# Decode attention with a gated MLP: early sum copied ahead of the late blocks, a share of the last key product on GpSimd, programs aligned to a block

## The chip, the cores and the metric

The kernel runs on one core of a Trainium2 chip. The metric is the device time of one execution in microseconds; the kernel before took 677.2 us (median of 3 runs, 676.89 to 677.97). A core has TensorE (PE) for matrix products, VectorE (DVE), ScalarE (ACT), GpSimd (POOL) and SyncE (SP), which here issues nearly all transfers. Sixteen DMA engines move the data from HBM into the on-chip memory SBUF; PE writes its sums to PSUM banks.

## The reference

Two inputs of one token each (B = 2, width 448) go through two branches that share x. Branch A is attention with a cache, branch B a two-layer MLP with a squared ReLU:

```python
q = (x @ wq).reshape(B, 1, 16, 256).transpose(0, 2, 1, 3)
scores = einsum("bhqd,bhkd->bhqk", q, k_cache) * 256 ** -0.5   # 4096 keys a head
o = einsum("bhqk,bhkd->bhqd", softmax(scores), v_cache)
a = o.transpose(0, 2, 1, 3).reshape(B, 1, 4096) @ wo
b = relu(x @ w1 + b1) ** 2 @ w2 + b2
g = sigmoid((x * gate_w).sum(-1, keepdims=True))
return g * a + (1 - g) * b
```

All is float32. The two caches are 2 x 16 x 4096 x 256 values each, 134 MB each; wq, wo, w1 and w2 are small beside them.

## The kernel before

**Rounds.** The attention goes in 16 rounds `r`, one for each pair of heads `t` (8) and each batch entry `b` (2). A round has 8.4 MB of keys and as much of values, laid over 128 partitions: 64 partitions a head, and 64 keys of 256 values (`KEYS` = 64, `DH` = 256) in each partition. The buffers are `keys[0]`, `keys[1]` (alternating) and `vals`.

**VectorE** (its loop is written out, L206 to L245): in each round it multiplies the keys in place with the broadcast query (L213), sums each product over 256 (the reduce of L222, 64 scores per partition), takes the maximum per partition (L223) and, after PE has spread it, over the head (L224). Between product and reduce stand two small steps for the round before (`normed`, L196 to L200). ScalarE then takes the exponentials (L240) into `p8` and the row sums. Ahead of the first rounds VectorE also does small steps for the gate and the hidden layer.

**PE** (L328 to the end, its own program): the gate's sum, q, the first layer of branch B (`fin`, L353 to L362), its transposes (L363 to L368), then the second layer summed into the bank `acc` by `add` (L371 to L374). A loop of 15 passes (L378 to L383) takes, for each round, the values times the exponentials into `po` (`values`, 32 calls), the scaling and turning of the result (`turn`), which ScalarE copies to `oT`, the next round's maxima and sums. The sixteenth round follows the loop (L386 to L390), because its values come in two parts into `keys[0]` (`V_CUT` = 48 of the 64 keys, semaphores `VT`).

**The last product, with wo** (L391 to L410). wo is 32 blocks of 128 x 448, loaded into `vals` in five cuts (`WO_CUTS` = 0, 16, 24, 28, 31, 32; semaphores `WL`), as soon as PE has read the values of the last round but one. The first 24 blocks ("early", 32 - `LATE`) go into the same bank `acc` as branch B, two columns wide, by `add`. Then ScalarE copies the sum to `ya` (L260). The last 8 blocks ("late") go to the bank `fin`, with the output's 448 columns split over four groups of PE's columns (`late`, four calls each); their left operands are copied by VectorE into the wide, zero-filled tile `wide` (L257 to L259). Halfway through the late blocks (`n == LATE // 2`), PE adds the early sum, by multiplying `ya` with the selection matrix `pick`. VectorE copies `fin` to `y4` (L261), and SP writes it out (L264).

**The order of the transfers** is that of SP's program: wq, the keys of round 0, the weights of branch B, then keys and values in turn, each waiting until its buffer has been read; at the end the last round's values, then the five cuts of wo. All of them go through one queue, so they land in that order.

GpSimd only sets up small tiles at the start and clears semaphores at the end (L266 to L270).

Of the kernel before, what the change touches and what calls it, by code (L numbers as in the profile page):

```python
# [7 lines left out]
ALU = mybir.AluOpType  # L8
AX = mybir.AxisListType

P = 128
WO_ORDER = [0, 1, 2, 3, 7, 4, 5, 6]
LATE = 8
WO_CUTS = (0, 16, 24, 28, 31, 32)
V_CUT = 48


class Count:
# [16 lines left out]
def gated_mix_kernel(nc, b2, wq, wf, wo, k_cache, v_cache, out):  # L35
    B, H, S, DH = k_cache.shape
# [5 lines left out]
    KEYS = 2 * S // P  # L42
# [11 lines left out]
    pe, dve, act, pool, sp = nc.tensor, nc.vector, nc.scalar, nc.gpsimd, nc.sync  # L54
    rounds = [(t, b) for t in range(T) for b in range(B)]
    R = len(rounds)

    def sb(name, *free):
        return nc.alloc_sbuf_tensor(name, [P, *free], F32)[:]
# [12 lines left out]
    pick = sb("pick", W)  # L72
    wide = sb("wide", LATE, W)
    p8 = sb("p", NM, 4)
# [12 lines left out]
    ya = sb("ya", D)  # L87
# [6 lines left out]
    DV, AC, TE, GP = (Count(nc, n) for n in ("dve", "act", "pe", "pool"))  # L94
    KL = [Count(nc, "k0_landed"), Count(nc, "k1_landed")]
# [14 lines left out]
    def kv(cache, r):  # L110
        t, b = rounds[r]
        return cache[b, 2 * t:2 * t + 2].rearrange("h (p j) d -> (h p) (j d)", j=KEYS)

    def load(dst, src, sem, after=None):
        ins = sp.dma_start(dst, src)  # L115
        if after:
            after[0].on(ins, after[1])
        return sem.up(ins, 16)
# [10 lines left out]
    def te_mt(r):  # L129
        return TE_MT0 if r == 0 else TE_SUM0 + 4 * (r - 1) + 3  # L130

    def te_sum(r):
        return TE_SUM0 if r == 0 else TE_SUM0 + 4 * (r - 1) + 4

    def te_val(r):
        return TE_SUM0 + 4 * r + 1

    def te_ot(r):
        return TE_SUM0 + 4 * r + 2

    TE_ACC = te_ot(R - 1) + 1
    TE_FIN = TE_ACC + 1


    pool.memset(ident, 0.0)
    GP.up(pool.memset(ones, 1.0))
# [37 lines left out]
    AC_QB = [AC.up(TE.on(act.activation(qb[:, i, :], QBANK[i % 4], AF.Copy), TE_QB[i])) for i in range(T * B // 2)]  # L184
# [6 lines left out]
    def turned(r):  # L191
        t, b = rounds[r]
        OC.up(TE.on(act.activation(o, po, AF.Copy), te_val(r)))  # L193
        AC_OT[r] = AC.up(TE.on(act.activation(oT[:, t, :, b, :], ot[:, :NJ * 2].rearrange("p (j h) -> p j h", h=2), AF.Copy), te_ot(r)))  # L194

    def normed(r):  # L196
        b = rounds[r][1]
        n = DV.up(TE.on(dve.reciprocal(rc, sm[:, :2]), te_sum(r)))
        RL.up(DV.on(dve.scalar_tensor_tensor(rl, rc.unsqueeze(1).to_broadcast([P, 2, 2]), gP[:, 0, b:b + 1],
                                             sel.rearrange("p (s h) -> p s h", s=2), op0=ALU.mult, op1=ALU.mult), n))  # L200

    def k_view(r):
        return keys[r % 2].rearrange("p (j d) -> p j d", d=DH)

    load(keys[1], kv(k_cache, 1), KL[1], (TE, TE_Q1))
    for r, (t, b) in enumerate(rounds):  # L206
        kt = k_view(r)
        q = qb[:, (t // 2) * B + b, (t % 2) * DH:(t % 2 + 1) * DH]
        if r < 4:
            dve.wait_ge(AC.h, AC_QB[(t // 2) * B + b])  # L210
        elif r == 4:
            dve.wait_ge(AC.h, AC_QB[-1])
        n = DV.up(KL[r % 2].on(dve.tensor_tensor(kt, kt, q.unsqueeze(1).to_broadcast([P, KEYS, DH]), op=ALU.mult), 16 * (r // 2 + 1)))  # L213
        if r == 0:
            DV_H = DV.up(TE.on(dve.tensor_tensor(hb, sm[:, :FC * B].rearrange("p (c b) -> p c b", b=B), b1T.unsqueeze(2).to_broadcast([P, FC, B]), op=ALU.add), TE_PT))
            DV_H = DV.up(DV.on(dve.tensor_scalar(hb, hb, 0.0, None, op0=ALU.max), DV_H))
            DV_H = DV.up(DV.on(dve.tensor_mul(hT, hb, hb), DV_H))
            DV_H = DV.up(DV.on(dve.tensor_tensor(hT, hT, gP[:, 1, :].unsqueeze(1).to_broadcast([P, FC, B]), op=ALU.mult), DV_H))
            load(vals, kv(v_cache, 0), VL, (TE, TE_ADD))
        else:  # L220
            normed(r - 1)
        DV_S = DV.up(DV.on(dve.tensor_reduce(s, kt, axis=AX.X, op=ALU.add), n))  # L222
        MX.up(DV.on(dve.tensor_reduce(m, s, axis=AX.X, op=ALU.max), DV_S))  # L223
        DV_NB = DV.up(TE.on(dve.tensor_reduce(nb, mt[:, :64], axis=AX.X, op=ALU.max, negate=True), te_mt(r)))  # L224
        if r > 0:
            turned(r - 1)
            if r < R - 1:
                load(vals, kv(v_cache, r), VL, (TE, te_val(r - 1)))
            else:
                for i, (lo, hi) in enumerate(zip(WO_CUTS, WO_CUTS[1:])):  # L230
                    load(vals[:, lo * D:hi * D], wo[:, lo * D:hi * D], WL[i], (TE, te_val(r - 1)) if i == 0 else None)
        if r + 2 < R:
            load(keys[r % 2], kv(k_cache, r + 2), KL[r % 2], (DV, DV_S))
        elif r + 2 == R:
            at = V_CUT * DH
            load(keys[r % 2][:, :at], kv(v_cache, R - 1)[:, :at], VT[0], (DV, DV_S))
            load(keys[r % 2][:, at:], kv(v_cache, R - 1)[:, at:], VT[1])
        for hh in range(2):
            z = slice(64 * hh, 64 * hh + 64)
            e = act.activation(p8[z, :, hh:hh + 3:2], s[z].rearrange("p (m s) -> p m s", s=2), AF.Exp,  # L240
                               bias=nb[z], accum_out=rsm[z, hh:hh + 1])
            if hh == 0:
                DV.on(e, DV_NB)
            else:
                EX.up(e)  # L245
# [3 lines left out]
    blocks = [(t, k) for t in WO_ORDER for k in range(4)]  # L249
    early = len(blocks) - LATE  # L250

    def o_block(t, k):
        hh, j = divmod(k, 2)
        return oT[:, t, j, :, hh]

    dve.wait_ge(AC.h, AC_OT[R - 1])
    for n, (t, k) in enumerate(blocks[early:]):  # L257
        DV_W = dve.tensor_copy(wide[:, n, 0:W:16], o_block(t, k))  # L258
    DV_W = DV.up(DV_W)  # L259
    AC_YA = AC.up(TE.on(act.activation(ya, acc[:, :D], AF.Copy), TE_ACC))  # L260
# [12 lines left out]
    def mm(dst, lt, rhs, start=True, stop=True):  # L273
        return pe.matmul(dst, lt, rhs, start=start, stop=stop)  # L274
# [7 lines left out]
    def done(ins, n):  # L282
        ins.then_inc(TE.h, 1)
        te[0] += 1
        assert te[0] == n, (te[0], n)

    def values(v, lo=0, hi=NM):
        vv = v.rearrange("p (m s d) -> p m (s d)", s=2, d=DH)
        for i in range(lo, hi):
            g = 32 * (i % 4)  # L290
            ins = mm(po[g:g + 4, :], p8[:, i, :], vv[:, i, :], i < 4, i >= NM - 4)
        return ins

    def turn():
        take(OC)
        take(RL)
        for j in range(NJ):
            for x in range(2):
                at = x * DH + j * P
                ins = mm(ot[:, j * 2:j * 2 + 2], o[:, at:at + P], rl[:, x, :], x == 0, x == 1)  # L300
        return ins
# [11 lines left out]

    n_acc = 1 + FC + T * 4 - LATE
    added = [0]

    def add(lt, rhs):
        n = added[0]
        g = 32 * (n % 4)
        added[0] += 1  # L320
        return mm(acc[g:g + B, :D], lt, rhs, n < 4, n >= n_acc - 4)

    def late(lt, rhs, start=False, stop=False):
        for k in range(4):
            ins = mm(fin[32 * k:32 * k + W, :DQ], lt, rhs[:, k * DQ:(k + 1) * DQ], start, stop)
        return ins
# [5 lines left out]
    for c in range(CF + 1):  # L332
        for n in range(4 * QW):
# [3 lines left out]
            else:  # L337
                half, i = divmod(n, 2 * QW)
                lt, at = xT[:, CF + half, :], CF * N + i * QB
            ins = mm(pq[a][32 * gq:32 * gq + B, :], lt, wqt[:, at:at + QB], c == 0, c == CF)  # L340
# [13 lines left out]
    for c in range(CF + 1):  # L354
        for n in range(4):
            if c < CF:
                lt, at = xT[:, c, :], c * F + n * D
            else:
                half, i = divmod(n, 2)
                lt, at = xT[:, CF + half, :], CF * F + i * D  # L360
            ins = mm(fin[32 * n:32 * n + B, :D], lt, vals[:, at:at + D], c == 0, c == CF)
# [4 lines left out]
    for n in range(2):  # L366
        ins = mm(sm[64 * n:64 * n + 64, CF * 8:CF * 8 + 4], hs[:, CF * P:D], rows[:, 2 * n:2 * n + 2, :B])
# [4 lines left out]
    for c in range(FC):  # L372
        ins = add(hT[:, c, :], vals[:, w2_at + c * D:w2_at + (c + 1) * D])
# [12 lines left out]
    pe.wait_ge(VT[0].h, 16)  # L386
    values(keys[R % 2], 0, V_CUT // 2)
    pe.wait_ge(VT[1].h, 16)
    done(values(keys[R % 2], V_CUT // 2, NM), te_val(R - 1))
    done(turn(), te_ot(R - 1))  # L390
    pe.wait_ge(AC.h, AC_OT[R - 1])  # L391
    i_w = 0
    for i, (t, k) in enumerate(blocks):
        if i == WO_CUTS[i_w]:
            pe.wait_ge(WL[i_w].h, 16)
            i_w += 1
        rhs = vals[:, i * D:(i + 1) * D]
        if i < early:
            ins = add(o_block(t, k), rhs)
            if i == early - 1:  # L400
                done(ins, TE_ACC)
            continue
        n = i - early
        if n == 0:
            pe.wait_ge(DV.h, DV_W)
        if n == LATE // 2:
            pe.wait_ge(AC.h, AC_YA)
            late(pick, ya)
        ins = late(wide[:, n, :], rhs, n == 0, n == LATE - 1)
    done(ins, TE_FIN)  # L410


# [63 lines left out]
```

## Time and profile before

| | |
|---|---|
| median of 3 runs (lowest, highest) | 677.2 us (676.89, 677.97) |
| the profiled execution, its own time | 676.97 us |
| its span, first to last instruction | 675.6 us |
| TensorE clock granted, mean | 0.653 |
| VectorE busy | 566.4 us, 84% |
| PE busy | 215.6 us, 32% |
| ACT, POOL busy | 36.2 us, 2.1 us |
| read from HBM | 289.55 MB, 429 GB/s over the span |

The profile is of one execution. Its times are microseconds from the start of the span unless marked ns. A row of the timeline gives start, length, engine, source line, operation, what it writes and reads, how often (x), and in brackets the idle time of the engine before it with what ended that. L274 and L115 are lines of helpers (`mm`, `load`), so their rows are told apart by the tiles. PEld is PE's loading of weights. Queue q1 carries the kernel's data; queues of the kind "instruction" carry program code to the engines.

### The profile page before, as it was taken

What the parts mean: (1) busy time and instruction counts of PE and PEld (TensorE: products, weight loads), DVE (VectorE), ACT (ScalarE), POOL (GpSimd) and SP (SyncE); (2) the same over time, 40 slices, a digit from 0 to 9 for tenths busy, and PEclk for the clock granted to TensorE, in tenths of its full rate; (3) what the DMA queues carried; (4) which work ended last, traced back from release to release, by engine and by line L of the source; (5) the groups of instructions that cost most, each with busy time, mean ns of one, the idle gap of its engine ahead of it and who ended that gap; (6) DMA issues with size and microseconds to landing.
All of it is one profiled execution on the core that took longest, in us unless ns stands there. A gap on an engine that the chain in (4) does not pass through costs nothing. (4 is left out here: it accounts for less than half of the span.)

```text
span 675.6 us, 3473 instructions
## 1 busy us (share of the span) xinstructions
PE 215.6 (32%) x1522; PEld 67.6 (10%) x1522; DVE 566.4 (84%) x120; ACT 36.2 (5%) x111; POOL 2.1 (0%) x15
## 2 busy tenths in 40 slices
PE   0726141150605124060503305050421405051357
PEld 0201000010101101010100101010010101011012
DVE  1066999999989797998979798997979799797960
ACT  0121000000000000000000000000000000000000
POOL 1000000000000000000000000000000000000000
PEclk9976666575756657585755658575565858565579
DMA  9999999999999999999999999999999999999997
GB/s 381 431 453 421 435 435 436 435 431 435 435 435 435 435 431 435 435 435 435 435 435 435 435 435 435 431 435 435 435 431 435 435 435 435 435 435 435 423 418 293
DMA packets 5779, 289.63 MB, mean 429 GB/s; under 512 B 653, under 2 KB 782, under 8 KB 1038
## 3 DMA queue, kind: packets, MB, share of 16 engines
q1 hardware_dynamic: 5772, 289.56, 99.2%
q8 instruction: 3, 0.05, 0.0%
q14 instruction: 2, 0.02, 0.0%
q10 hardware_dynamic: 2, 0.00, 0.0%
HBM read 289.55 MB, written 0.00 MB: 429 GB/s over the span
## 5 line engine op out<-in xcount | busy, mean ns | idle before, releaser
L213 DVE TENSOR_TENSOR k<-k,q 128x16384 f32<-128x16384 f32 x16 | 275.6, 17223 | 51.7 <-DMA k<-in_k_cache_dram 51.7
L222 DVE TENSOR_REDUCE s<-k 128x64 f32<-128x16384 f32 x16 | 275.4, 17212 | 0.0
L274 PE MATMUL po<-v,p 128*4 128x512 f32 x960 | 137.4, 737 | 291.4 <-PEq L278 291.4
L274 PEld LDWEIGHTS po<-v,p 128*4 128x4 f32 x960 | 26.6, 99 | 389.5 <-issue 389.5
L274 PE MATMUL mt<-ident,m 128*64 128x64 f32 x64 | 7.7, 334 | 88.8 <-PEq L278 88.8
L193 ACT ACTIVATE o<-po 128x512 f32<-128x512 f32 x16 | 9.6, 597 | 449.8 <-PE po L274 449.8
L274 PE MATMUL ot<-rl,o 128*128 128x2 f32 x128 | 16.4, 250 | 15.6 <-PEq L278 15.6
L274 PEld LDWEIGHTS ot<-rl,o 128*128 128x128 f32 x128 | 15.5, 191 | 30.0 <-issue 30.0
L240 ACT ACTIVATE p<-s,nb 64x64 f32<-64x64 f32 x32 | 11.2, 350 | 104.8 <-DVE nb L224 104.6
L274 PE MATMUL sm<-rsm,ones 128*128 128x2 f32 x32 | 8.9, 348 | 21.2 <-PEq L278 21.2
L274 PEld LDWEIGHTS mt<-ident,m 128*64 128x64 f32 x64 | 5.2, 205 | 90.4 <-issue 90.4
L174 DVE COPY pk<-k 128x28 f32<-128x28 f32 x1 | 0.2, 179 | 16.5 <-DMA k<-in_wq_dram 16.5
L224 DVE TENSOR_REDUCE nb<-mt 128x1 f32<-128x64 f32 x16 | 3.6, 224 | 10.6 <-PE mt L274 10.6
L274 PE MATMUL fin<-v,pk 128*2 128x448 f32 x32 | 6.0, 933 | 16.6 <-DMA v<-in_wf_dram 16.6
L274 PEld LDWEIGHTS sm<-rsm,ones 128*128 128x128 f32 x32 | 8.0, 310 | 23.8 <-issue 23.8
L258 DVE COPY wide<-oT 128x2 f32<-128x2 f32 x8 | 0.7, 162 | 10.4 <-ACT oT L194 10.4
L274 PE MATMUL pq<-k,pk 128*2 128x512 f32 x64 | 9.3, 747 | 0.0
L274 PE MATMUL po<-k,p 128*4 128x512 f32 x64 | 8.7, 702 | 0.0
L274 PE MATMUL sm<-ys,ones 128*128 128x2 f32 x2 | 0.6, 350 | 21.0 <-DVE ys L177 21.0
L261 DVE COPY y<-fin 128x112 f32<-128x112 f32 x1 | 0.3, 275 | 7.7 <-PE fin L274 7.7
L240 ACT ACTIVATION_READ_ACCUMULATOR p<-s,nb 64x1 f32 x32 | 5.9, 184 | 0.0
L274 PE MATMUL acc<-v,oT 128*2 128x448 f32 x48 | 4.9, 538 | 0.4 <-ACT oT L194 0.3
(59 smaller groups left out, 58.2 us busy)
## 6 DMA issues: line engine op xcount, KB each, us to landing
k<-in_wq_dram SPq DMA_DIRECT2D x1, 7182.0 KB, 19.6
v<-in_wf_dram SPq DMA_DIRECT2D x1, 6272.0 KB, 52.8
k<-in_v_cache_dram SPq DMA_DIRECT2D x1, 6144.0 KB, 37.8
v<-in_wo_dram SPq DMA_DIRECT2D x1, 3584.0 KB, 18.6
k<-in_v_cache_dram SPq DMA_DIRECT2D x1, 2048.0 KB, 42.4
v<-in_wo_dram SPq DMA_DIRECT2D x1, 1792.0 KB, 22.6
v<-in_wo_dram SPq DMA_DIRECT2D x1, 896.0 KB, 24.3
v<-in_wo_dram SPq DMA_DIRECT2D x1, 672.0 KB, 25.4
```

The source lines that it names most:

```text
L174: DV_PK = DV.up(QL.on(dve.tensor_copy(pk, keys[1][:, 3 * N + N // 2:3 * N + N // 2 + PK]), 16))
L193: OC.up(TE.on(act.activation(o, po, AF.Copy), te_val(r)))
L213: n = DV.up(KL[r % 2].on(dve.tensor_tensor(kt, kt, q.unsqueeze(1).to_broadcast([P, KEYS, DH]), op=ALU.mult), 16 * (r // 2 + 1)))
L222: DV_S = DV.up(DV.on(dve.tensor_reduce(s, kt, axis=AX.X, op=ALU.add), n))
L224: DV_NB = DV.up(TE.on(dve.tensor_reduce(nb, mt[:, :64], axis=AX.X, op=ALU.max, negate=True), te_mt(r)))
L240: e = act.activation(p8[z, :, hh:hh + 3:2], s[z].rearrange("p (m s) -> p m s", s=2), AF.Exp, bias=nb[z], accum_out=rsm[z, hh:hh + 1])
L258: DV_W = dve.tensor_copy(wide[:, n, 0:W:16], o_block(t, k))
L261: DV_Y4 = DV.up(TE.on(dve.tensor_copy(y4, fin[:, :DQ]), TE_FIN))
L274: return pe.matmul(dst, lt, rhs, start=start, stop=stop)
```

## The change

Three edits, told apart here as part 1, 2 and 3.

Part 1: `LATE` goes from 8 to 4, so 28 blocks are early. PE waits for the copy `ya` and multiplies it with `pick` ahead of the first late block, not halfway; that product now opens the sum in `fin`. The wait for VectorE's copies into `wide` stands right behind the last early block.

Part 2: in the last round (r = 15) VectorE multiplies 54 of the 64 keys, GpSimd the other 10 (`HELP`), both released by the keys' landing. VectorE's reduce waits for GpSimd.

Part 3: a directive at the head of PE's program puts its next instruction on a boundary of 256 instructions, and one at the head of VectorE's on a boundary of 128; `max_nops=0` has the program branch over the padding.

```diff
-LATE = 8
+LATE = 4
...
+HELP = 10
...
+    dve.addr_align(128, 0, max_nops=0)
+    pe.addr_align(256, 0, max_nops=0)
...
-        n = DV.up(KL[r % 2].on(dve.tensor_tensor(kt, kt, q.unsqueeze(1).to_broadcast([P, KEYS, DH]), op=ALU.mult), 16 * (r // 2 + 1)))
+        own = KEYS if r < R - 1 else KEYS - HELP
+
+        def times_q(e, lo, hi):
+            return KL[r % 2].on(e.tensor_tensor(kt[:, lo:hi], kt[:, lo:hi], q.unsqueeze(1).to_broadcast([P, hi - lo, DH]), op=ALU.mult), 16 * (r // 2 + 1))
+
+        n = DV.up(times_q(dve, 0, own))
+        if own < KEYS:
+            pool.wait_ge(AC.h, AC_QB[-1])
+            GP_HELP = GP.up(times_q(pool, own, KEYS))
...
             normed(r - 1)
+        if own < KEYS:
+            dve.wait_ge(GP.h, GP_HELP)
         DV_S = DV.up(DV.on(dve.tensor_reduce(s, kt, axis=AX.X, op=ALU.add), n))
...
     for i, (t, k) in enumerate(blocks):
+        if i == early:
+            pe.wait_ge(AC.h, AC_YA)
+            late(pick, ya, True)
         if i == WO_CUTS[i_w]:
             pe.wait_ge(WL[i_w].h, 16)
             i_w += 1
...
             if i == early - 1:
                 done(ins, TE_ACC)
+                pe.wait_ge(DV.h, DV_W)
             continue
         n = i - early
-        if n == 0:
-            pe.wait_ge(DV.h, DV_W)
-        if n == LATE // 2:
-            pe.wait_ge(AC.h, AC_YA)
-            late(pick, ya)
-        ins = late(wide[:, n, :], rhs, n == 0, n == LATE - 1)
+        ins = late(wide[:, n, :], rhs, False, n == LATE - 1)
```

## The prediction

> **What bounds the kernel now.** I read the page first, for the share of each engine and of the DMA.
>
> ```profile
> span 675.6 us, 3473 instructions
> PE 215.6 (32%) x1522; PEld 67.6 (10%) x1522; DVE 566.4 (84%) x120; ACT 36.2 (5%) x111; POOL 2.1 (0%) x15
> ...
> q1 hardware_dynamic: 5772, 289.56, 99.2%
> q8 instruction: 3, 0.05, 0.0%
> q14 instruction: 2, 0.02, 0.0%
> ```
>
> The data queue fills 99.2% of the time of 16 DMA engines. VectorE, the busiest compute engine, has 84%, and none of the 289.56 MB is touched by the change. So only two things can move the time: when the last byte lands, and what comes behind it. The chain that ended last, in order of time, says the same:
>
> ```profile
> 646.88 25.45 DMA v<-in_wo_dram
> 672.33 0.04 issue
> 672.37 1.20 PE fin L274 x40
> 673.57 0.02 issue
> 673.59 0.28 DVE y L261
> ```
>
> The chain waits for wo until 672.33 us, then come 40 matmuls (1.20 us), one copy and the output's DMA. The table of windows shows how the stream ends (columns: stretch, length, busy time of PE, PEld, DVE, ACT and POOL, granted clock, DMA share, GB/s):
>
> ```profile
> 665.00:670.00 5.00, 4.66 (x48) 1.05 (x48) 0.66 (x8) 0.17 (x1) 0.00 (x0) 1.00 1.00 413
> ...
> 671.00:671.50 0.50, 0.50 (x28) 0.41 (x20) 0.00 (x0) 0.00 (x0) 0.00 (x0) 1.00 0.33 133
> 671.50:672.00 0.50, 0.17 (x8) 0.00 (x0) 0.00 (x0) 0.00 (x0) 0.00 (x0) 1.00 0.20 75
> 672.00:672.30 0.30, 0.00 (x0) 0.00 (x0) 0.00 (x0) 0.00 (x0) 0.00 (x0) 1.00 0.16 60
> 672.30:672.60 0.30, 0.23 (x12) 0.23 (x16) 0.00 (x0) 0.00 (x0) 0.00 (x0) 1.00 0.05 18
> ```
>
> The 16 DMA engines do not end together: from 671.0 about 5 of them work (0.33 x 16), and up to 672.3 fewer than 3 (0.16 x 16 = 2.6). Those few stragglers set the end. Could all end together, the stream would be over near 671.0, some 1.3 us sooner.
>
> **Part 1: early sum first, four late blocks.** The timeline of the end, in order:
>
> ```profile
> 654.32 8.67 PE L274 MATMUL po<-k,p 128*4 128x512 f32 x64
> 665.25 4.97 PE L274 MATMUL acc<-v,oT 128*2 128x448 f32 x48 [0.26 <-ACT oT L194]
> 667.13 0.10 PEld L274 LDWEIGHTS acc<-v,oT 128*2 128x2 f32 x4 [0.27 <-issue]
> 667.50 0.10 PEld L274 LDWEIGHTS acc<-v,oT 128*2 128x2 f32 x4 [0.27 <-issue]
> 668.53 0.11 PEld L274 LDWEIGHTS acc<-v,oT 128*2 128x2 f32 x8 [0.92 <-DMA v<-in_wo_dram]
> 670.28 0.54 ACT L260 ACTIVATE ya<-acc 128x448 f32<-128x448 f32 x1 [5.09 <-PE acc L274]
> 670.71 0.96 PE L274 MATMUL fin<-v,wide 128*17 128x112 f32 x32 [0.49 <-DMA v<-in_wo_dram]
> 672.37 0.39 PE L274 MATMUL fin<-ya,pick 128*17 128x112 f32 x8 [0.70 <-DMA v<-in_wo_dram]
> 672.57 0.95 PE L274 MATMUL fin<-v,wide 128*17 128x112 f32 x32
> ```
>
> Each call of a matmul is two matmul and two weight-load instructions (64 for the 32 calls of `values`). Today the third cut of wo lets PE go on at 670.71, the fourth at 672.37; behind the fourth stand the 8 matmuls on `pick` and 32 on the last four blocks, 1.20 us for 40, so 0.03 us each at most. Taking those 8 out from behind the landing is worth 0.2 us by that quotient and 0.1 us if only the gap to the next group counts (their 0.39 us ends well past the start of the next ones); I take 0.1.
>
> Whether they really come ahead: blocks 24 to 27 now go to `acc` once the third cut is there. Four such blocks are two groups 0.375 us apart (667.13 to 667.50, rounded). The last group began at 669.65 (three steps of 0.375 behind 668.53) and ACT's copy at 670.28, so 0.63 from the last group to the copy. From 670.71: 670.71 + 0.375 + 0.63 = 671.71, copy until 672.25, a semaphore and `pick`'s matmuls (0.05 + 0.1): PE is through at about 672.40, against 672.37 at which the fourth cut releases it. So 0.03 of the 0.1 is lost again: **-0.07 us**. Bounds: -0.2 (all 8 hidden), +0.2 (copy and `pick` a little later still). VectorE's copies into `wide` fall from 8 to 4, at 665.2, beside PE.
>
> **Part 2: ten of 64 keys to GpSimd.** VectorE's two long passes of the last round:
>
> ```profile
> 616.93 17.22 DVE L213 TENSOR_TENSOR k<-k,q 128x16384 f32<-128x16384 f32 x1 [2.87 <-DMA k<-in_k_cache_dram]
> ...
> 634.41 17.21 DVE L222 TENSOR_REDUCE s<-k 128x64 f32<-128x16384 f32 x1
> ```
>
> The multiply loses 10/64 of 17.22 = 2.69 us and takes 14.53. If GpSimd works beside it, the reduce starts at 631.7, and everything behind it (maximum, exponentials, values from 654.32, `ot`, `oT`) 2.7 us sooner. That buys nothing: PE already ran out of wo ahead of 668.53 (0.92 idle, released by the DMA), and would only wait longer for the same landings. The new wait of VectorE for GpSimd stands ahead of the reduce; queued behind it are the two maxima, and ACT and PE wait for those.
>
> How late may this chain become? With 28 early blocks there are 14 groups. Run from 665.25 without a wait, the last would begin 13 x 0.375 = 4.88 later, at 670.13, while the third cut lets it begin at 670.71 + 0.375 = 671.09 at the earliest. So 0.96 us of delay are free; beyond that each microsecond counts in full. GpSimd's product is therefore hidden as long as it is through by 634.1 + 0.96 = 635.1.
>
> What it takes alone is not in the trace. The nearest rows:
>
> ```profile
> 0.87 0.10 POOL L146 MEMSET ones<- 128x1 f32 x1
> ...
> 1.40 0.99 POOL L153 COPY v<-ident 128x128 f32<-128x128 f32 x4
> ```
>
> A copy of 128 elements is 0.25 us, 0.10 of it fixed by the memset of one element: 1.2 ns per element, or 1.9 with the fixed part in. 2560 elements are 3.1 us with one input, 6.1 with two inputs, 9.9 with two and nothing taken off. I take 6.1, as the product reads two. Beside VectorE it would end near 623 (627 at the worst), far below 635.1, and even running at a third of that speed it ends in time. Cost: **0**, under cover of the wo stream.
>
> The rule that speaks against this edit: the Trainium skill, "SBUF — State Buffer", section "Who interferes with whom", has a VectorE instruction with two SBUF inputs contend with a GpSimd instruction that reads SBUF, and the second to issue wait for the whole of the first. No instruction of this trace shows such a pair; what it would do is the first rival.
>
> **Part 3: aligned programs.** The instruction fetches are DMA packets too. In the two windows 58 to 60 us and 668 to 670 us, and in a third near 104:
>
> ```profile
> q8 instruction: 1, 0.02, 3.1%
> ...
> q8 instruction: 1, 0.02, 3.4%
> ```
>
> 3.4% of 16 engines for 2 us is 1.09 us of one engine. An engine with a fetch is that much behind with its data for good, since nothing leaves the stream idle: three PE fetches, and just under three engines at work at the end. Counting four instructions a call and one for each wait, move or branch, PE's program has 337 ahead of the loop, 164 in it, 396 behind. Fetches 256 apart (the size named in the change) fit all three if they are called at about instructions 176, 432 and 688: the first `fin` matmuls, the loop's first values, the early adds from 665.25, each some 3.5 us ahead of its packet.
>
> ```profile
> 55.18 5.35 PE L274 MATMUL fin<-v,pk 128*2 128x448 f32 x28
> ```
>
> Aligned, they would be called at 0, 256, 512 and 768: at the start, at the transposes of `hs` (near 60 us), in the last `values` (654.32, so a packet near 658) and at `pick` (after 672, when the stream is through). Two within the stream instead of three, VectorE's own (q14) moved to the start, but still two, each holding an engine for 1.09 us; the last engine ends as late as today. **0**, with bounds of 1.3 less (no straggler left) and 1.09 more (a fetch on an engine that already has one).
>
> The branch over the padding runs while both engines have nothing to do, 16.48 and 21.04 us long:
>
> ```profile
> 20.31 0.18 DVE L174 COPY pk<-k 128x28 f32<-128x28 f32 x1 [16.48 <-DMA k<-in_wq_dram]
> ...
> 21.04 0.56 PE L274 MATMUL sm<-ys,ones 128*128 128x2 f32 x2 [21.04 <-DVE ys L177]
> ```
>
> **Sum.** -0.07 + 0 + 0 against the profiled execution's 676.97 (span 675.6 and 1.4 around it) is 676.9. That execution lies 0.2 below the median of the runs, 677.2, so I forecast 677.1 for a median. About 0.2% (1.35 us) is what a measurement of this kernel can tell from no change.
>
> **Rivals.**
>
> *The two products run one after the other* (slower). Both are released by the same landing, at 616.93. If one holds the other off, the products take 14.53 + 6.1 = 20.63 us instead of 17.22, and the reduce starts 3.4 us later, whichever goes first. Less the free 0.96, that is +2.4: 679.5. With GpSimd's bounds of 3.1 and 9.9 us: 677.1 to 683.3. It decides from 3.65 us of GpSimd work on (17.22 + 0.96 - 14.53). For it: a GpSimd instruction has never run beside a VectorE multiply in this trace, so nothing shows that it can. Against it: nothing in the trace shows a hold either. The Trainium skill, "GPSIMD Engine Reference", section "Elementwise — side-by-side cycle accounting", gives 4497 ns for 2048 elements of two inputs; by that the product is 5.6 us (an estimate) and the rival's time 679.0. Chance 0.27.
>
> *The stragglers shrink* (faster). If the moved fetches leave no engine behind, the fourth cut lands up to 1.3 us sooner: 675.7 to 676.0. For it: fewer than 3 engines are the last. Against: two fetches remain inside the stream. Chance 0.12, of which about two thirds clear the 1.35 us bound with the 0.07 to 0.2 of part 1 or with the spread of the runs.
>
> *A fetch hits an engine that is late already*: +1.09, 678.2, mostly within 0.2%. Chance 0.06.
>
> *The alignment does nothing* (padding present, fetches as before) gives the forecast, and is in its chance.
>
> **Numbers.** Forecast 677.1, chance 0.55, its own range 676.2 to 678.0 (part 1's bounds and the runs' spread of 676.89 to 677.97). The range for 8 in 10 takes in the stragglers' case down to 675.8 and the serial case up to 679.6; above it lie only GpSimd speeds near the worst row. Slower: 0.26 of the serial case and 0.01 of the rest, 0.27. Faster: 0.08 and 0.02 of the forecast's lower edge, 0.10. Same: 0.63.
>
> **What would show it.** Right: the multiply of VectorE near 14.5 us and GpSimd's beginning with it; last `values` starting near 651.7; PE's wait ahead of the second wo cut longer than 0.92; no q8 packet from 668 to 671; the fourth cut again releasing PE near 672.4, with 32 and not 40 matmuls behind it. Wrong: GpSimd's product beginning at 631.5, or VectorE's lasting 20 us; `acc` starting after 666.2; a DMA share that falls from 1.0 to 0 in less than 1 us at the end, or a last landing beyond 673.

## The result, and the profile after

The changed kernel takes 679.07 us (median of 13 runs, 678.53 to 681.55) against 677.2 for the kernel before (13 runs of the same session, 676.76 to 678.24). The ratio is 1.0036, 95% interval 1.0027 to 1.0046: slower by some 2.4 us, where no difference was forecast (the means, 679.84 and 677.40, are that far apart; the medians are 1.9 apart). The time is inside the range given for 8 in 10 and on the side of the first rival (679.5 by rows). The Trainium skill's figure gave 679.0 for that rival.

The times of both kernels fall into two groups: before, 7 of 13 up to 677.2 and 6 from 677.85 to 678.24; after, 8 of 13 from 678.53 to 679.19 and 5 from 681.16 to 681.55. What parts the groups is the subject of the later experiments; the two profiles compared here, 676.97 and 678.87 us, both belong to the lower one. The groups are not always so clean: of 35 runs of the kernel before beside the first four experiments, 7 lie between them, from 677.33 to 677.84. One execution of a later experiment (part 2 alone) was in a slow state, 894.22 us, and is left out of its figures.

The page of the changed kernel, its lines on GpSimd's new instruction and the queues:

```profile
span 677.4 us, 3425 instructions
...
q1 hardware_dynamic: 5772, 289.56, 99.0%
q8 instruction: 4, 0.07, 0.0%
q14 instruction: 2, 0.02, 0.0%
...
L220 POOL TENSOR_TENSOR k<-k,q 128x2560 f32<-128x2560 f32 x1 | 19.9, 19937 | 614.2 <-DMA k<-in_k_cache_dram 614.2
```

GpSimd's product lasts 19.94 us, 7.8 ns for each of 2560 elements. The timeline of the last round shows where that time goes:

```profile
616.88 14.56 DVE L220 TENSOR_TENSOR k<-k,q 128x13824 f32<-128x13824 f32 x1 [2.86 <-DMA k<-in_k_cache_dram]
616.94 19.94 POOL L220 TENSOR_TENSOR k<-k,q 128x2560 f32<-128x2560 f32 x1 [614.22 <-DMA k<-in_k_cache_dram]
631.36 0.16 DVE L202 RECIPROCAL rc<-sm 128x2 f32<-128x2 f32 x1
631.56 5.33 DVE L203 SCALAR_TENSOR_TENSOR rl<-rc,gP,sel 128x4 f32<-128x4 f32 x1
636.98 17.22 DVE L236 TENSOR_REDUCE s<-k 128x64 f32<-128x16384 f32 x1
```

VectorE's product has its full speed (14.56 us, forecast 14.53). GpSimd's row begins with it but ends 5.44 us behind it, at 636.88. And the little step on `rl`, four elements a partition and 0.22 us in the kernel before, takes 5.33 and ends together with GpSimd's product. In the kernel before it was:

```profile
634.27 0.22 DVE L199 SCALAR_TENSOR_TENSOR rl<-rc,gP,sel 128x4 f32<-128x4 f32 x1
```

Read as one picture, which the experiments below test: while VectorE's product runs, GpSimd stands although its row counts as busy; then GpSimd works 5.44 us, and VectorE's next instruction with two operands in SBUF stands. The reduce starts at 636.98, not 634.41.

What comes of it at the end, in the chain that ended last:

```profile
667.72 0.18 ACT oT L198
667.90 0.04 issue
667.95 5.49 PE acc L288 x56
673.44 0.02 issue
673.46 0.55 ACT ya L274
674.01 0.14 issue
674.15 1.19 PE fin L288 x40
675.34 0.02 issue
675.36 0.28 DVE y L275
```

No DMA stands in it any more. PE sums 28 blocks from 667.95 without a wait, ScalarE copies, and only then come `pick` and the four late blocks, long after the data are there (stretch, length, busy PE, PEld, DVE, ACT, POOL, granted clock, DMA share, GB/s):

```profile
671.50:672.00 0.50, 0.50 (x10) 0.10 (x4) 0.00 (x0) 0.00 (x0) 0.00 (x0) 1.00 0.19 72
672.00:672.30 0.30, 0.30 (x8) 0.10 (x4) 0.00 (x0) 0.00 (x0) 0.00 (x0) 1.00 0.16 60
672.30:672.60 0.30, 0.30 (x8) 0.10 (x4) 0.00 (x0) 0.00 (x0) 0.00 (x0) 1.00 0.00 0
```

The stream ends as before, with the same few stragglers, near 672.3. `acc` starts 2.70 us later than before (667.95 against 665.25), of which 0.96 was free: 1.74 are left, and VectorE's last copy indeed starts 1.77 us later (675.36 against 673.59).

### The profile page after: what moved, and what is told of

Read it like the earlier page. It is cut to its first block, busy times and chain, and to the rows that moved or that the text cites. A ratio compares the mean times of both kernels' runs of the same rounds, so it can differ in the third digit from the quotient of the medians.

```text
span 677.4 us, 3425 instructions
## 1 busy us (share of the span) xinstructions
PE 214.3 (32%) x1498; PEld 67.2 (10%) x1498; DVE 568.7 (84%) x116; ACT 36.1 (5%) x111; POOL 22.0 (3%) x16
## 5 line engine op out<-in xcount | busy, mean ns | idle before, releaser
L220 DVE TENSOR_TENSOR k<-k,q 128x16384 f32<-128x16384 f32 (+1 forms) x16 | 272.9, 17057 | 51.3 <-DMA k<-in_k_cache_dram 51.3
L220 POOL TENSOR_TENSOR k<-k,q 128x2560 f32<-128x2560 f32 x1 | 19.9, 19937 | 614.2 <-DMA k<-in_k_cache_dram 614.2
L203 DVE SCALAR_TENSOR_TENSOR rl<-rc,gP,sel 128x4 f32<-128x4 f32 x16 | 8.7, 542 | 0.6
```

The costliest lines, as they stand in the source:

```text
L220: return KL[r % 2].on(e.tensor_tensor(kt[:, lo:hi], kt[:, lo:hi], q.unsqueeze(1).to_broadcast([P, hi - lo, DH]), op=ALU.mult), 16 * (r // ...
```

## The experiments

The theories. **S**: the product of VectorE and that of GpSimd exclude each other; the loss is that alone, and falls due because the chain has only 0.96 us of room. **P**: GpSimd is that slow (7.8 ns an element) beside any work of VectorE's. **F**: parts 1 or 3 carry some of the loss. Ratios are to runs of the kernel before on the same chip, whose median was 677.51 us beside the first four experiments, 677.24 beside the next four and 677.30 beside the last two.

**Part 2 taken back.**

```diff
-HELP = 10
+HELP = 0
```

> The changed kernel without part 2: VectorE multiplies all 64 keys of the last round, GpSimd none. Parts 1 and 3 stay. Theory S (the two products exclude each other: VectorE's 14.56 us, then GpSimd's 5.4, so the reduce starts at 636.98 and not at 634.4, and all of the loss is that): 676.9 to 677.2, the reduce near 634.4, acc again waiting for the second wo cut, PE released near 672.4 by the fourth. Rival F (parts 1 or 3 carry part of the loss): 677.9 or more.

Measured: 678.27 us (11 runs, 677.21 to 679.3), ratio 1.0008 (1.0000 to 1.0017). The reduce is back at 634.41:

```profile
634.41 17.21 DVE L236 TENSOR_REDUCE s<-k 128x64 f32<-128x16384 f32 x1
```

Most of the loss is gone, but the median is above what S gave and, by its number, where F put it (677.9 or more): six of the eleven lie at 678.3 to 679.3, the profiled one among them (679.03). Its PE rows:

```profile
654.32 9.94 PE L288 MATMUL po<-k,p 128*4 128x512 f32 x64
665.24 1.02 PE L288 MATMUL ot<-rl,o 128*128 128x2 f32 x8 [0.98 <-PEq L292]
666.53 7.14 PE L288 MATMUL acc<-v,oT 128*2 128x448 f32 x56 [0.26 <-ACT oT L198]
674.42 0.39 PE L288 MATMUL fin<-ya,pick 128*17 128x112 f32 x8 [0.76 <-ACT ya L274]
```

The same work is slower: 9.94 us for the last values (8.67 in the profile of the kernel before) and 7.14 for the 56 matmuls into `acc`, 5.44 in the changed kernel's. The granted clock is the third number from the right in the table of windows; first this run, then the kernel before:

```profile
658.00:662.00 4.00, 4.00 (x32) 0.74 (x28) 0.00 (x0) 0.00 (x0) 0.00 (x0) 0.73 1.04 441
662.00:666.00 4.00, 3.02 (x31) 1.13 (x24) 0.00 (x0) 0.60 (x1) 0.00 (x0) 1.00 0.95 401
666.00:670.00 4.00, 3.74 (x27) 1.06 (x30) 0.38 (x4) 0.17 (x1) 0.00 (x0) 0.63 0.97 403
```

```profile
658.00:662.00 4.00, 4.00 (x44) 0.91 (x40) 0.00 (x0) 0.00 (x0) 0.00 (x0) 1.00 0.94 405
662.00:666.00 4.00, 2.76 (x29) 1.23 (x25) 0.66 (x8) 0.77 (x2) 0.00 (x0) 1.00 0.96 409
666.00:670.00 4.00, 3.91 (x44) 0.84 (x36) 0.00 (x0) 0.00 (x0) 0.00 (x0) 1.00 0.98 401
```

The clock differs in two places: it rises later during the last values (0.73 against 1.00 from 658 to 662), and it falls behind them (0.63 against 1.00 from 666 to 670). In this execution the chain outlasts the data even without part 2. That the fall, which comes in some executions only, makes the upper group is taken up below as theory **C**.

**Part 2 alone** (the kernel before, 10 keys for GpSimd as in the change, nothing else).

> The kernel before with part 2 alone: 24 early and 8 late blocks, pick halfway, no alignment. Theory S with an interplay of parts 1 and 2: the reduce again starts near 637.0 and acc near 667.95, but only 24 blocks are summed ahead of the copy (last of 12 groups at 672.08, copy 672.7 to 673.25, while PE does four late blocks until 673.2), then 40 matmuls until 674.5: 678.2, half of the loss. If the sharing costs the same whatever the tail is: 679.0.

Measured: ratio 1.0022 (1.0010 to 1.0034), median of 11 runs 678.35; the lower group (6) lies at 677.6 to 678.35, as forecast for an interplay with the tail, the upper one (5) at 680.1 to 681.0. Both groups lie under those of the changed kernel (678.5 to 679.2 and 681.2 to 681.6), so the same delay seems to cost less with 24 early blocks than with 28; the intervals of the two ratios overlap. Its profile, one of the upper group (680.09), shows a reason:

```profile
674.56 0.94 PE L286 MATMUL fin<-v,wide 128*17 128x112 f32 x32
675.50 0.39 PE L286 MATMUL fin<-ya,pick 128*17 128x112 f32 x8
675.69 0.96 PE L286 MATMUL fin<-v,wide 128*17 128x112 f32 x32
```

PE does four late blocks while ScalarE copies, and goes on to `pick` without a wait. With part 1 it has nothing to do during that copy (the 0.76 us of idle time in the row of `pick` above), and four more blocks stand ahead of the copy.

**Part 1 alone** (`LATE = 4` and the new order; all keys on VectorE, no directive).

> The kernel before with part 1 alone (early sum ahead of four late blocks; all keys on VectorE, no alignment). Theory S: 677.1, that is 0.07 less than before, PE through pick near 672.4. Rival F: 677.9 or more, pick's copy ending well after the fourth wo cut.

Measured: ratio 1.0001 (0.9993 to 1.0010), median 677.09, with 6 of 11 from 676.9 to 677.1 and 5 from 678.2 to 678.9. The profiled execution is again of the upper group (678.26; clock 0.60 from 666 to 670):

```profile
665.81 7.09 PE L286 MATMUL acc<-v,oT 128*2 128x448 f32 x56 [0.26 <-ACT oT L196]
673.67 0.39 PE L286 MATMUL fin<-ya,pick 128*17 128x112 f32 x8 [0.77 <-ACT ya L272]
673.86 0.96 PE L286 MATMUL fin<-v,wide 128*17 128x112 f32 x32
```

There is neither a gain nor a loss that can be measured; the forecast gain of 0.07 is below what these runs resolve.

**Part 3 alone.**

```diff
+    dve.addr_align(128, 0, max_nops=0)
+    pe.addr_align(256, 0, max_nops=0)
```

> The kernel before with part 3 alone. Theory S: 677.2 within 0.3; instruction packets of PE near 2, 64 to 68, 657 to 661 and after 671 us, and no packet of VectorE's between 150 and 250; the last wo cut lands within 0.2 us of the kernel before. Rival F: 677.9 or more.

Measured: ratio 1.0005 (0.9997 to 1.0014), median 677.9: no change that can be told, though the median is 0.4 above the 677.51 of the kernel before beside it. The profiled execution, 678.16, is the nearest there is to a profile of the kernel before in its upper group, since its tail is the same. The clock is 0.50 from 667 to 669, and PE's 48 matmuls into `acc` take 6.33 us, not 4.97, with no wait for wo behind them:

```profile
666.28 6.33 PE L277 MATMUL acc<-v,oT 128*2 128x448 f32 x48 [0.26 <-ACT oT L197]
```

The packets moved as counted: one within 656 to 660 us,

```profile
q8 instruction: 1, 0.02, 1.6%
```

1.6% of 16 engines over 4 us, 1.0 us of one engine, as for the fetches before; the others lie at the start, near 70 and past 672. The end of the stream did not come sooner. So neither part alone shows the loss that F asks for; the two together, in the run with part 2 taken back, leave up to 0.17% open.

**Who holds whom: VectorE's query from PSUM.** The bank `pq[1]` still holds the last query. In the last round VectorE reads it there, so that only the keys come from SBUF; GpSimd's product is unchanged.

```diff
         def times_q(e, lo, hi):
-            return KL[r % 2].on(e.tensor_tensor(kt[:, lo:hi], kt[:, lo:hi], q.unsqueeze(1).to_broadcast([P, hi - lo, DH]), op=ALU.mult), 16 * (r // 2 + 1))
+            qv = pq[1][:, DH:] if e is dve and r == R - 1 else q
+            return KL[r % 2].on(e.tensor_tensor(kt[:, lo:hi], kt[:, lo:hi], qv.unsqueeze(1).to_broadcast([P, hi - lo, DH]), op=ALU.mult), 16 * (r // 2 + 1))
```

> The changed kernel, but VectorE's product of the last round reads its query from a PSUM bank that still holds it; GpSimd's ten keys stay as they are. So VectorE reads one operand from SBUF, not two. Theory S (two SBUF inputs of VectorE and GpSimd's reads exclude each other): GpSimd's product takes about 5.5 us from 616.9 and not 19.9, VectorE's 14.5 to 14.6, the small step on rl 0.2 and not 5.3, the reduce starts near 631.7, acc near 664.2 with the first wo cut: 676.9 to 677.2. Rival P (GpSimd is that slow by itself beside any VectorE work, 7.8 ns an element): again 19.9 us and 679.

Measured: ratio 1.0005 (0.9996 to 1.0014), median 677.72. The timeline of the last round:

```profile
617.02 14.55 DVE L221 TENSOR_TENSOR k<-k,pq 128x13824 f32<-128x13824 f32 x1 [2.86 <-DMA k<-in_k_cache_dram]
617.07 5.61 POOL L221 TENSOR_TENSOR k<-k,q 128x2560 f32<-128x2560 f32 x1 [614.36 <-DMA k<-in_k_cache_dram]
631.69 0.22 DVE L203 SCALAR_TENSOR_TENSOR rl<-rc,gP,sel 128x4 f32<-128x4 f32 x1
631.83 17.21 DVE L237 TENSOR_REDUCE s<-k 128x64 f32<-128x16384 f32 x1
```

With that one operand moved, both products run side by side, GpSimd's in 5.61 us (5.62 and 5.61 in the two later profiles with this edit), and the step on `rl` has its 0.22 again. P is refuted, S holds: what stood in the way is the operand that VectorE's second read takes from SBUF. That both engines read one query tile is not the reason, since the step on `rl` was held too and reads neither query nor keys. The loss of part 2 is gone, the rest of the change kept. The tail also gives the size of part 1 where the chain comes early:

```profile
671.82 0.54 ACT L275 ACTIVATE ya<-acc 128x448 f32<-128x448 f32 x1 [8.15 <-PE acc L289]
672.51 0.39 PE L289 MATMUL fin<-ya,pick 128*17 128x112 f32 x8 [0.76 <-ACT ya L275]
```

`pick` begins 0.15 us behind the copy, at 672.51. That it would be through by 672.40 was some 0.2 us too hopeful, so nothing is won by moving it.

**Twice the share.**

```diff
-HELP = 10
+HELP = 20
```

> The changed kernel with 20 keys for GpSimd. Theory S (first VectorE, 44 keys in 11.84 us, then GpSimd at the 0.545 us a key of the changed kernel's 5.45 us behind VectorE's end): GpSimd through at 616.9 + 11.9 + 10.9 = 639.7, the reduce 2.7 us later than with 10 keys, the end 681.6. Rival P (7.8 ns an element throughout): GpSimd 39.9 us, the reduce at 656.9, the end near 699.

Measured: one execution of 684.04 us.

```profile
616.81 11.89 DVE L220 TENSOR_TENSOR k<-k,q 128x11264 f32<-128x11264 f32 x1 [2.88 <-DMA k<-in_k_cache_dram]
616.87 22.68 POOL L220 TENSOR_TENSOR k<-k,q 128x5120 f32<-128x5120 f32 x1 [614.15 <-DMA k<-in_k_cache_dram]
628.82 10.74 DVE L203 SCALAR_TENSOR_TENSOR rl<-rc,gP,sel 128x4 f32<-128x4 f32 x1
639.65 17.22 DVE L236 TENSOR_REDUCE s<-k 128x64 f32<-128x16384 f32 x1
```

GpSimd ends 10.85 us behind VectorE's product, twice the 5.44 of ten keys, and the reduce starts at 639.65 as S has it (39.9 us by P). The end is 2.4 us later than S gave (681.6): `acc` took 7.14 us here, not 5.44, and the last values 9.58, not 8.79, together 2.5. So this single execution also has the fall of the clock.

**Part 2 alone, query from PSUM** (24 early and 8 late blocks as before).

> The kernel before with the shared product alone (10 keys), VectorE's query from PSUM. Theory S: reduce near 631.7, acc from 664.2, 676.8 to 677.1 in all executions, because the chain has 2.6 us more room when the granted clock of PE halves between 666 and 670; so the group of executions near 678.2 that the kernel before has goes away, and the median is up to 0.5 under it. If that second group does not come from PE's clock: it stays, and the median is that of before.

Measured: median 676.96, all 11 runs from 676.77 to 677.74; ratio 0.9998 (0.9988 to 1.0007). Of the 27 runs of the kernel before beside it, 10 lie at 677.87 or more, of these none. Three runs (677.14, 677.67, 677.74) lie above the 677.1 that was forecast for all. Its profile has the fall of the clock, and it does no harm (676.83 us):

```profile
662.00:666.00 4.00, 2.79 (x20) 1.40 (x24) 0.66 (x8) 0.20 (x2) 0.00 (x0) 0.77 0.98 416
666.00:670.00 4.00, 4.00 (x39) 0.86 (x32) 0.00 (x0) 0.00 (x0) 0.00 (x0) 0.81 0.97 395
```

**The same with five matmuls on spare data** around the last turn.

> As the one with the old tail and the query from PSUM, and five matmuls of 128 x 512 on spare data around the last turn, while PE waits for ScalarE and for wo. If PE's clock in the tail falls because of that pause: clock 1.00 from 663 to 673 in the profile and no execution above 677.3. If the fall has another cause: as without them, or later by their 2.2 us less the room.

Measured: median 676.96, 676.78 to 677.39, two of 11 runs above the 677.3 of the forecast; ratio 0.9995 (0.9986 to 1.0004). The clock is 1.00 from 658 to 674. The times are no better than without the matmuls: the room that the shared product gives is enough by itself.

**Theory C by itself: the kernel before with two such matmuls.**

```diff
+    mm(pq[0], ident, qb[:, 0, :])
     done(turn(), te_ot(R - 1))
+    mm(pq[0], ident, qb[:, 1, :])
     pe.wait_ge(AC.h, AC_OT[R - 1])
```

> The kernel before with two matmuls of 128 x 512 on spare data, one ahead of the last turn and one behind it, while PE waits for ScalarE (some 0.5 us more on the path to acc, inside the free 0.96). Theory C (the executions of the kernel before near 678 are those in which PE's granted clock halves between 664 and 670, because PE does next to nothing from 663 to 666): clock 1.00 from 662 to 673 in the profile, no execution above 677.6, median 676.9 to 677.1. Rival (the clock's fall does not hang on this pause, or the late group comes from elsewhere): a third or more of the executions stay at 677.8 to 678.4.

Measured: median 677.11, 676.79 to 677.47; ratio 0.9996 (0.9987 to 1.0005). Of the 15 runs of the kernel before beside it, 5 lie from 677.94 to 678.29. None of the eleven runs is in the upper group, and the profile has the full clock, as the one profile of the kernel before had, so it is the eleven times that speak for C:

```profile
662.00:666.00 4.00, 4.00 (x24) 1.58 (x16) 0.57 (x8) 0.77 (x2) 0.00 (x0) 1.00 0.98 416
666.00:670.00 4.00, 4.00 (x45) 1.16 (x48) 0.09 (x2) 0.00 (x0) 0.00 (x0) 1.00 0.98 402
```

**And the changed kernel with them.**

> The changed kernel with the same two matmuls. Its chain has no room, so they cost up to 0.5 us in every execution. Theory C: the executions near 681.4 go away, all lie between 678.7 and 679.6. Rival: about 5 of 13 stay above 681.

Measured: 680.15, five runs of 679.05 to 680.45; ratio 1.0037 (1.0023 to 1.0050). None is above 681, as C has it, but four are above 679.6: the forecast is half missed. Five runs are also few: that the changed kernel's upper group (5 of 13) goes with the pause is not shown. In the profile the last values took 9.68 us, not 8.79 (the clock was at a half until 662, and the matmuls behind the values cannot change that), and `acc` started 1.52 later than in the changed kernel's own profile, 0.6 of it by the two matmuls:

```profile
656.90 9.68 PE L288 MATMUL po<-k,p 128*4 128x512 f32 x64
...
669.47 5.44 PE L288 MATMUL acc<-v,oT 128*2 128x448 f32 x56
```

On this path, which has no room, filling the pause won nothing (ratio 1.0037 against 1.0036).

## Why the prediction was wrong

**The step that failed** is that of part 2: "Beside VectorE it would end near 623 (627 at the worst), far below 635.1, and even running at a third of that speed it ends in time. Cost: 0". The length was right: 5.61 us were measured once nothing held GpSimd, between the rows' 3.1 and 9.9 and near the 6.1 taken. What was not true is "beside": VectorE's product and GpSimd's ran one after the other, 14.56 us and then 5.44, and the reduce started at 636.98. The cost was 1.8 us at the end of the chain, not 0. That is what the Trainium skill's "SBUF — State Buffer", section "Who interferes with whom", has for a VectorE instruction with two SBUF inputs and a GpSimd instruction that reads SBUF: the trace agrees, in both directions (GpSimd held for 14.5 us, then VectorE's small step for 5.33), and the query in PSUM takes the conflict away. No row of the old trace could show it; the rival was given 0.27, and the weight lay on the absence of a row that showed a hold. The reserve, "a third of that speed", was no cover either: three times 6.1 from 616.93 ends at 635.2, past the prediction's own 635.1, and the row in fact lasted 19.94.

Two of its signs could not tell the cases apart. GpSimd's row does begin with VectorE's (its sign of being right) and not at 631.5 (its sign of being wrong), because the row counts the time in which GpSimd is held. What told it was `acc`, which started after 666.2, at 667.95, and the last values, which started at 656.90 and not near 651.7.

**The rival's sum** held but for sizes. Delay of the reduce: 3.4 forecast, 2.57 measured, since GpSimd's part was 5.44 us and not 6.1 and VectorE's two small steps fall into the wait. The free 0.96 us was right: 2.70 of delay at `acc`, 1.77 at the end. That the rival's +2.4 by rows equals the 2.4 of the ratio is luck: the two profiles differ by 1.9, and the rest has another cause. The Trainium skill's 4497 ns for 2048 elements ("GPSIMD Engine Reference", "Elementwise — side-by-side cycle accounting") gives 5.62 us for 2560 (an estimate); 5.61 were measured.

**What the sum left out** is PE's clock. It took "each microsecond counts" from one execution in which the clock was 1.00 behind 658. In others it falls to a half for some 3 us, behind a stretch of 2.3 us (662.99 to 665.25 in the kernel before) in which PE waits for ScalarE or multiplies two columns wide. In some it also rises later during the last values. The kernel before has an upper group about 1.0 us later (676.9 and 678.0), the changed one 2.5 (678.8 and 681.4). No execution of either upper group was profiled, so the size for the changed kernel is an estimate from the run with twice the share: without room, its values (9.58 for 8.79) and its `acc` (7.14 for 5.44) both count in full and make 2.5. That would be why the ratio, 2.4 us, is larger than the 1.9 between the profiles.

For the tail of the kernel before, the runs show that the upper group goes when the pause is filled or the chain has room. None of 11 executions is in it in each of three experiments (old tail with the query from PSUM, the same with five matmuls, the kernel before with two), against 5 of 15 and 10 of 27 of the kernel before beside them. That the pause is what lowers the clock is the likeliest reading and not more. Of the nine profiles without the filling, seven show a fall that begins between 664 and 672; of the three with it, none does. The Trainium skill ("TensorE: Matmul & The Clock Gate", "What's actually happening") sets the clock by how busy PE has lately been, in windows that run freely of the program; that would also make it a matter of chance for one and the same kernel, as here.

**Part 1**: 0 within 0.1%, as forecast; the 0.07 us of gain is not there, by the 0.15 us from copy to `pick` and the copy's own lateness. What was missed is that it probably makes the tail less tolerant: the copy is no longer covered by late blocks.

**Part 3**: the fetches went where the count put them (near 2, 68, 661 and past 675 us in the changed kernel; forecast were the start, one called near 60, a packet near 658 and one after 672, the last two now later with the whole chain), and the end of the stream did not move, as forecast. The link that the prediction drew from three fetches to just under three last engines is not borne out: with two of PE's fetches inside the stream instead of three, the DMA share from 671 to 672.3 is the same (0.33, 0.19, 0.16 against 0.33, 0.20, 0.16).

## What to carry to other kernels

Before a share of an elementwise step goes to GpSimd, count the SBUF operands of the VectorE instructions that run meanwhile, the small ones too: with two, the engines took turns here, and a product that is "busy" in the profile may only be waiting. A PSUM copy of the small operand made the split work, though here it removes no more than the late executions of the upper group, since the transfers set the end. A change to a tail that is hidden by a stream should be judged by the room it leaves, in more than one execution, not by its place in one profile.

## What the runs showed of the hardware that was not expected

- A GpSimd row's length contains the time in which it is held: 19.94 us for 5.4 us of work, 22.68 for 10.8.
- A four-element step on VectorE was held for 5.33 and 10.74 us by GpSimd.
- PE's granted clock in the last 10 us differs from one execution to the next of one program, and a tail that is off the critical path in one profile is on it in the next.
